# Attention with a gated MLP on one core: the score and pooling stages of pairs 2 and 3, the form of batch 0's v and u products, and a new order of all tasks

## The chip, the core and the metric

The kernel runs on one core of one Trainium2 chip. A core has TensorE (matrix products into PSUM), VectorE (DVE in the profile), ScalarE (ACT), GpSimd (POOL) and SyncE (SP), which issues the transfers between the chip's memory and SBUF. Each engine works through its own list of instructions in order; semaphores tie the lists together. The metric is the device time of one execution in microseconds (us), the median of three runs; a profiled execution is one more run with its own time.

## The reference, cut to what matters

Eight batches; for each, eight heads of 576 positions and 64 dimensions. An attention over pooled q, k, v (groups of four positions) and a local one (positions less than four apart) are added and give x of 576 x 512. A gated MLP follows.

```python
factor = 4; Sd = 144; scale = 1 / 8
q_d = q.reshape(B, H, Sd, factor, D).mean(axis=3)      # k_d, v_d likewise
out_up = np.repeat(sm_attn(q_d, k_d, v_d), factor, axis=2)
mask = np.abs(pos[:, None] - pos[None, :]) < factor
attn = softmax(np.where(mask, scale * q @ k.T, -1e9))
x = out_up + attn @ v                                   # (B, S, H * D)
h = gelu(x @ w_in)                                      # 512 -> 1024
u, v = h[..., :512], h[..., 512:]
v_n = (v - mu) / np.sqrt(var + 1e-06) * g_ln
v_s = np.einsum('ts,bsd->btd', w_sg, v_n) + b_sg[None, :, None]
out = x + (u * v_s) @ w_out
```

## The kernel before

Two heads make a pair; there are 32 pairs, four to a batch, numbered 0 to 31 over all batches. `attention(b, p)` makes the tasks of a pair, `mlp(b)` those of a batch. All tensors lie transposed so that a pair fills 128 partitions.

A pair g runs through these tasks: `lq`, `lk`, `lv`, `lw` load q, k, v in pooling form (`v4`) and v in window form (`vw`); `qs` and `ks` sum q and k over four positions; `S` (L617) is the local score product, 20 plain fp32 products of 64 x 64 x 64, and `Y` (L643) the pooled one; `mx`, `nx`, `my`, `ny` take maxima and biases; `ea`, `eb`, `ec` are the exps; `re`, `rc` sum and invert; `np`, `nq` normalise; `T`, `U`, `t` turn the probabilities on TensorE and `pa` to `pe` evict them; `D` (L782, task `av`) multiplies them with v; `oe`, `od`, `xa`, `xb` put both attentions together into x of this pair.

Three constants set a form for the first pairs. For g < EARLY_S the mask goes into PSUM by two bf16 products ahead of the scores, and S and Y are two tasks; later pairs have one task `YS` (both products) and VectorE adds the mask (`ma`, `mb`). For g < EARLY_D the pooled product runs over four slices of v instead of over their sum; later pairs sum v first (`vs`, two adds for each half on GpSimd or one reduce for each on VectorE, L606). For g < WIDE there is one exp over all ten tiles with the maxima subtracted beforehand (`ia`, `ib`) and the row sums taken by VectorE (`es`); later pairs have ten small exps with a bias each. All three constants are 4.

The MLP products keep fp32 accuracy by splitting each operand into a high and a low part of type fp32r and adding three products. So x gets `xh`, `xl` (its halves) and `xc` (the last 64 positions of the low half beside the high ones), and each weight block, which arrives as float64, is rebuilt (`wu`, `wq`, `wb`, `wt`) and then split (`wh`, `wl`). `v0.s` is the product for 128 positions by 512 columns (L906), 12 products, for the last 64 positions 8, whose two halves `va`, `vj` add; for batch 0 it is cut into quarters by pair (`vk s.k`). `u0.i` (L1117) is 12 products of 128 x 128 x 288. Then follow gelu (`vg`, `ua`), the statistics (`vb`, `vp`, `vn`), the spatial product `s`, the gate, and the output product `o`. From batch 1 on, s and o use sums of blocks with fewer products, whose weights are prepared once (`zf` to `zl`, `ta` to `tl`, `be`, `bs`, `gt`) between batch 0 and 1.

The order is written out by hand: ORDER names every task, and `/V`, `/A`, `/P` choose its engine where the first one listed isn't meant. `place` (L66) hands out buffers in that order: eight PSUM banks, ten wide buffers X, 38 buffers R. The list sets each engine's order and SyncE's; a transfer also waits for the sixth one before it (DEPTH). A load can wait for a task: `lv` of the pairs up to 5 waits for D of two pairs before, `lw` for D of four pairs before. WARM (L211) puts products of zeros ahead of S0 (28) and S3 (20).

## Time and profile before

| | us |
|---|---|
| median of three runs (lowest, highest) | 561.27 (560.44, 561.32) |
| the profiled execution's own time | 562.39 |
| its span, first to last instruction | 560.6 |
| TensorE busy | 536.9 (96%) |
| VectorE busy | 483.5 (86%) |
| ScalarE busy | 417.4 (74%) |
| GpSimd busy | 364.0 (65%) |
| mean granted TensorE clock | 0.994 of full |

The span is divided into stretches below. Times in the rows are microseconds unless marked ns. PE is TensorE, PEld its loading of stationary operands (which overlaps it), PEclk the granted clock as a share of 2.4 GHz. Ends of TensorE's products are modelled, so the spacing of products in a dense run says what one costs, and the mean of one says how long it takes from start to end. "issue" as a releaser means that the profile shows nothing that the engine waited for.

### The profile page before, as it was taken

Reading aid. Unit: us, or ns where it says so; the run is one execution under the profiler, and the core shown is the slowest. Engines: PE = TensorE matmul, PEld = TensorE weight load, DVE = VectorE, ACT = ScalarE, POOL = GpSimd, SP = SyncE. Lnnn points to the kernel's source line nnn. Section 1 sums busy time; section 2 is a strip of 40 time slices with the busy share of each in tenths; the row PEclk is TensorE's granted clock in tenths of the full one; section 3 lists DMA queues with packets and bytes.
Section 4 is the critical chain, followed back from the end, with each engine's and each line's share of the span. In section 5 each row is a group of like instructions: output and inputs, shape, how many; then the busy total and the mean of one; then the engine's idle time right before and its main releaser. Section 6 shows DMA issues by size and latency. Waiting matters only on the chain.

```text
span 560.6 us, 17562 instructions
## 1 busy us (share of the span) xinstructions
PE 536.9 (96%) x6864; PEld 499.9 (89%) x6864; DVE 483.5 (86%) x1008; ACT 417.4 (74%) x1384; POOL 364.0 (65%) x441
## 2 busy tenths in 40 slices
PE   6858999999989999999999999999999999999997
PEld 5656899989989899989998899989999899989997
DVE  8967899999999999897879887897889988777665
ACT  4974899989978788679777789784976797735412
POOL 5992988895576776567648288737847665535314
PEclk9988999999999999999999999999999999999999
DMA  8789529123553053141432323411344133100103
GB/s 314 237 234 318 170 82 278 53 67 105 158 176 122 2 154 110 47 136 42 157 108 77 100 90 122 155 45 57 118 144 135 36 101 109 50 1 2 64 21 107
DMA packets 31923, 64.50 MB, mean 115 GB/s; under 512 B 3808, under 2 KB 4832, under 8 KB 31840
## 3 DMA queue, kind: packets, MB, share of 16 engines
q1 hardware_dynamic: 31840, 63.37, 36.0%
q8 instruction: 54, 0.88, 0.7%
q14 instruction: 29, 0.24, 0.1%
HBM read 53.92 MB, written 9.44 MB: 113 GB/s over the span
## 4 chain that ended last, share of the span: by engine, by line
PE 82%; DVE 8%; DMA 6%; issue 3%; ACT 1%; SPq 1%; DVEq 0%; ACTq 0%
PE ps L1114 19%; PE ps L916 17%; PE ps L1068 16%; PE ps L1243 14%; PE ps L792 4%; PE ps L808 3%; PE ps L629 3%; PE ps L731 3%; DMA R<-in_qT_dram 3%; PE ps L650 2%; PE ps L740 2%; DMA R<-in_kT_dram 1%; DMA weight_z<-in_w_in_dram 1%; DMA weight_y<-in_w_in_dram 1%; SPq L240 1%
## 5 line engine op out<-in xcount | busy, mean ns | idle before, releaser
L1114 PE MATMUL ps<-X,weight_z 128*128 128x288 f32 x512 | 109.2, 298 | 1.6 <-DVE X L637 1.6
L916 PE MATMUL ps<-weight_y,X 128*128 128x512 f32 x320 | 97.3, 398 | 0.1
L689 ACT ACTIVATE X<-X,nb 128x64 f32<-128x64 f32 x280 | 93.6, 339 | 1.2 <-DVE nb L668 0.8
L1114 PEld LDWEIGHTS ps<-X,weight_z 128*128 128x128 f32 x512 | 84.1, 188 | 2.2 <-DVE X L637 1.8
L1114 PE MATMUL ps<-R,weight_z 128*128 128x288 f32 x256 | 75.5, 295 | 0.0
L916 PEld LDWEIGHTS ps<-weight_y,X 128*128 128x128 f32 x320 | 58.5, 188 | 12.7 <-ACT R L1142 0.4
L1068 PE MATMUL ps<-wsg_h,R 128*128 128x288 f32 x266 | 58.4, 300 | 0.3 <-ACT pd L711 0.3
L248 ACT CAST R<-R 128x576 fp32r<-128x576 f32 (+2 forms) x77 | 48.0, 646 | 13.7 <-DVE R L1105 5.9
L1250 DVE TENSOR_TENSOR R<-ps,R 128x288 f32<-128x288 f32 x98 | 41.9, 448 | 16.8 <-PE ps L1243 16.6
L689 ACT ACTIVATION_READ_ACCUMULATOR X<-X,nb 128x1 f32 x280 | 53.4, 191 | 0.0
L248 ACT COPY R<-ps 128x464 f32<-128x464 f32 (+4 forms) x94 | 35.0, 412 | 23.2 <-PE ps L731 10.3
L1226 POOL TENSOR_TENSOR R<-R,R 128x576 fp32r<-128x576 f32 x24 | 35.2, 1477 | 26.2 <-ACT R L248 11.7
L916 PE MATMUL ps<-weight_y,R 128*128 128x512 f32 x128 | 50.6, 395 | 0.5 <-DVE R L827 0.5
L1243 PE MATMUL ps<-R,weight_r 128*128 128x288 f32 x336 | 50.3, 297 | 0.0
L1114 PEld LDWEIGHTS ps<-R,weight_z 128*128 128x128 f32 x256 | 48.2, 188 | 0.1
L1243 PEld LDWEIGHTS ps<-R,weight_r 128*128 128x128 f32 x336 | 46.7, 188 | 0.9
L1068 PEld LDWEIGHTS ps<-wsg_h,R 128*128 128x128 f32 x266 | 43.5, 188 | 0.9 <-ACT pd L711 0.6
L1243 PE MATMUL ps<-R,R 128*128 128x288 f32 x252 | 38.6, 299 | 0.8 <-DVE R L470 0.8
L1003 POOL TENSOR_TENSOR R<-R,R 128x512 fp32r<-128x512 f32 (+1 forms) x18 | 24.9, 1393 | 20.9 <-DVE R L248 7.6
L1142 ACT ACTIVATE R<-ps 128x288 f32<-128x288 f32 x64 | 24.5, 412 | 16.8 <-PE ps L1114 15.5
L1243 PEld LDWEIGHTS ps<-R,R 128*128 128x128 f32 x252 | 34.8, 188 | 1.7 <-DVE R L470 1.2
L711 ACT ACTIVATE pd<-ps,nbd 128x144 f32<-128x144 f32 x96 | 35.3, 377 | 0.9 <-DVE nbd L680 0.2
(215 smaller groups left out, 1624.2 us busy)
## 6 DMA issues: line engine op xcount, KB each, us to landing
R<-in_v_dram SPq DMA_DIRECT2D x56, 224.0 KB, 3.6
X<-in_vw_dram SPq DMA_DIRECT2D x32, 320.0 KB, 3.9
R<-in_kT_dram SPq DMA_DIRECT2D x32, 293.0 KB, 3.6
R<-in_qT_dram SPq DMA_DIRECT2D x32, 293.0 KB, 3.1
out_dram<-R SPq DMA_DIRECT2D x28, 288.0 KB, 3.0
R<-in_w_sgT_dram SPq DMA_DIRECT2D x10, 288.0 KB, 3.9
weight_y<-in_w_in_dram SPq DMA_DIRECT2D x4, 512.0 KB, 5.5
weight_z<-in_w_in_dram SPq DMA_DIRECT2D x4, 512.0 KB, 5.3
```

Source lines behind the costliest of these rows:

```text
L248: (nc.scalar.copy if e == "A" else ENG[e].tensor_copy)(**kw)
L689: nc.scalar.activation(out=st["ms"][:, t, :], in_=src, func=AF.Exp, bias=st["nb"][:, t:t + 1], scale=scale, accum_out=sums[par][:, t:t + 1])
L711: nc.scalar.activation(out=pd[:, n], in_=st["sdv"][n].rearrange("p (c k) -> p c k", c=3), func=AF.Exp, bias=st["nbd"][:, n:n + 1], scale=s ...
L792: nc.tensor.matmul(out=out, lhsT=lhsT, rhs=pdt[ks, probs, h * QC:(h + 1) * QC], start=first, stop=last)
L916: nc.tensor.matmul(out=acc, lhsT=r32(l), rhs=r32(weights[f"y{k}"][:, 0, w]), start=(i == 0 and ks[0] == 0), stop=(i == len(ops) - 1 and ks ...
L1003: ENG[e].tensor_tensor(out=r32(dst), in0=vact[s][0][0:n], in1=vh[0:n, 0:DM], op=ALU.subtract)
L1068: nc.tensor.matmul(out=s_bank(j, c), lhsT=r32(l), rhs=r32(r), start=first_in and i == 0, stop=i == len(ops) - 1, skip_group_check=not firs ...
L1114: nc.tensor.matmul(out=acc[:, 0:HALF], lhsT=r32(l), rhs=r32(r), start=(first and n == 0), stop=(last and n == len(ops) - 1))
L1142: nc.scalar.activation(out=gate(i), in_=at["ps", "m", b, "u", i][:, 0:HALF], func=AF.Gelu_apprx_tanh)
L1226: ENG[e].tensor_tensor(out=r32(gl[m]), in0=us[raws[m]], in1=gh[m], op=ALU.subtract)
L1243: nc.tensor.matmul(out=bank(j, c), lhsT=r32(l), rhs=r32(r), start=first and i == 0, stop=i == len(ops) - 1, skip_group_check=not first)
L1250: nc.vector.tensor_tensor(out=x, in0=bank(j, c), in1=x, op=ALU.add)
```

## The change

EARLY_S, EARLY_D and WIDE become 2: pairs 2 and 3 take the later pairs' form (`YS`, mask added by VectorE, ten small exps, v summed first). For batch 0, v and u become one plain fp32 product for each pair instead of three split ones, from x and the rebuilt weights as they are; batch 0 has no `xh`, `xl`, `xc`, and no `va`, `vj`. The low parts of the weights are waited for by batch 1 instead. `nq` may run on ScalarE as three scaled copies, `xc` on ScalarE. ORDER is new throughout; WARM is the same, but no task S3 is left. Over both orders, tasks change engines: `nq` 14 on ScalarE (none before), `xc` 10 on ScalarE (none before), `vb` 36 on ScalarE (29), `np` 25 on GpSimd (19), `qs` and `ks` 27 on GpSimd (21), `vs` 18 on VectorE (16), `pc` 16 on VectorE (10), `xl` 13 on GpSimd (19).

```diff
 ORDER = """
-wy0 wuy0 wqy0/V wby0 wty0 wz3 wqz3 wbz3 lk0 lq0 qs0 S0 mx0 lk1 lq1 S1 ks0/P Y0 lq2 ks1/P ia0 ib0 wuz3 wy1 ea0 mx1 wqy1
...
-wbz0 ea2 T1 pa1 pa0 wtz0 pb0 my2 pc0 small t0 pe0 wby2 wuy2 wty2 ny2 ec2 es2 my3 ny3/V U1 pb1 pc1/V re2 rc2 t1 whz0
-ks4/P ec3 pe1 D0 oe0 es3 wby1 re3 od0 nq2 why2 YS4 wy3 wuy3 lq5 np2 wqy3 qs5 lv2 U2 T2 pa2 wty1 xa0 rc3 why1 nq3 t3 xb0
-np3 wlz0 my4 ny4 t2 pb2/V wby3 ma4 pc2 lv1 lw1 xh0 xl0/P ec4 U3 wly2 T3 pa3 wty3 mb4 pb3/V wz2 pc3/V lk5 pe2 mx4 pe3 ks5
-wqz2 wbz2 wuz2 D1 YS5 ma5 my5 oe1 od1 xa1 xb1 mb5 lw2 mx5 wly0 D2 oe2/V lv4 od2 xh1/V lw3 vk1.0 vk2.0 nx4 eb4 ea4 re4
-rc4 lv3 D3 xa2 xl1 wtz2 whz2 wly1 vk1.1 nx5 vs4 ea5 eb5 xb2 xh2 ny5 nq4 wz1 oe3/V od3 xa3 xb3 xh3 xc0 why3 wly3 ec5
...
+lq0 lk0 ks0 qs0/P S0 mx0 lk1 ks1/P wy0 wqy0 Y0 my0 lq1 ia0 lq2 ib0 qs1/P ea0 ny0 qs2/P lk3 Y1 wby0 es0 my1 lq3 ec0 re0
+lk2 ks3/P S1 qs3 YS3 lv0 wuy0 mx1 wz3 rc0 ia1 ks2/P ib1 ma3 ny1 ec1 mb3 ea1 es1 re1 YS2 wy1 wuz3 mx3 nq0 ma2 t0 np0 T0
+nx3 wqz3 wz0 pa0 lw0 wty0 U0 rc1 ea3 lk4 nq1 mb2 mx2 np1 T1 pb0/V my3 my2 ny2/V wqy1/V wqz0/V ny3/V pc0/V pe0/V nx2 eb2
+lq5 why0/V lq4 t1 wy2 U1 ec2 wby1 lv1 ea2 ec3 re2 lw1 eb3 D0 pa1/V pb1 pc1 wbz0 ks4/P pe1 qs5/P rc2 np2/V lk5 re3/V rc3
+wuz0 nq3/A wqy2 wy3 T2 oe0/V od0 xa0 xb0 qs4/P YS4 ma4 np3 nq2 T3 pa3 wuy2 wtz0 mb4 mx4 nx4 whz0 pa2 wly0 lv2 D1 t2 U2
+ks5/P my4 ny4 wz1 wuy1 wby2 ec4 lv3 pb2 wty1 pc2/V pe2 oe1/V od1 wuy3 vk2.0 vk0.0 U3 vs2 ea4 eb4 xa1 xb1 pb3 pc3/V wty2
+wqy3/V YS5 t3 ma5 mb5 mx5 vk0.1 vk1.0 vs3 my5 ny5 vk3.0 wby3 ec5 vk2.1 vk1.1 pe3/V lw2 wbz3 wty3 why2 wtz3 nx5 D2 oe2/V
+wly2 od2 xa2 xb2 lw3 D3 oe3/V od3 vk3.1 xa3 wuz1 xb3 vk3.2 lq6 lv4 vk2.2 v0.2 re4 rc4 wz2 ea5 eb5 re5/V vk0.2 v0.0 rc5
...
 """
 DEPTH = 6
-EARLY_S, EARLY_D, WIDE, SMALL_O, SMALL_S = 4, 4, 4, 1, 1
+EARLY_S, EARLY_D, WIDE, SMALL_O, SMALL_S = 2, 2, 2, 1, 1
...
+    def unsplit(t):
+        return at["R", "w", t][:, 0:DM]
...
         def norm_d(e):
+            if e == "A":
+                for i in range(3):
+                    nc.scalar.activation(out=st["pdv"][:, i], in_=st["pdv"][:, i], func=AF.Copy,
+                                         scale=st["rc"][:, NT + i:NT + i + 1])
+                return
...
+        if b == 0:
+            return
         add(N("xh"), {"A": 0.64, "V": 0.4}, x_high, [N("xa"), N("xb")], takes=[("X", "xh", g)])
...
-        add(N("xc"), {"P": 0.27}, x_last, [N("xl")])
+        add(N("xc"), {"P": 0.27, "A": 0.25}, x_last, [N("xl")])
...
-        xn = [f"xl{b * NPAIR + p}" for p in range(NPAIR)]
+        xn = [f"{'xb' if first else 'xl'}{b * NPAIR + p}" for p in range(NPAIR)]
...
+                if first:
+                    for k in ks:
+                        l = sb[k]["x"][:, s * P:min(S, (s + 1) * P)]
+                        nc.tensor.matmul(out=acc[0:LEFT] if last else acc, lhsT=l, rhs=unsplit(f"y{k}"), start=k == 0, stop=k == KT - 1)
+                    return
...
+                if first:
+                    acc = buf("ps", "m", b, "u", i)[:, 0:HALF]
+                    for k in range(KT):
+                        l = block(unsplit(f"z{k // 2 * 2 + d}"))[:, k % 2, ds]
+                        nc.tensor.matmul(out=acc, lhsT=l, rhs=sb[k]["x"][:, cs], start=k == 0, stop=k == KT - 1)
+                    return
...
-            w = [f"wly{i}" for i in range(KT)] if first else []
+            w = [f"{'wty' if first else 'wly'}{i}" for i in range(KT)] if b < 2 else []
...
-            if last:
+            if last and not first:
                 add(N("va", s), {"A": 0.58, "V": 0.6}, v_act(s), [N("v", s)], takes=[("R", "v", b, s)])
...
+            z = [f"z{j}" for j in range(KT) if j % 2 == i // 4]
+            w = [f"{'wt' if first else 'wl'}{j}" for j in z] if b < 2 else []
```

## Rows read from the trace of the kernel before

**Rows 1.** Busy time of each engine by stage; the first line names the columns.

```profile
core 0: us, PE busy (x) PEld busy (x) DVE busy (x) ACT busy (x) POOL busy (x), PEclk, DMA share, GB/s
0.00:52.45 52.45, 37.14 (x854) 30.50 (x854) 40.27 (x106) 34.52 (x121) 38.02 (x52) 0.93 0.85 276
52.45:106.50 54.05, 54.05 (x764) 50.40 (x762) 48.64 (x109) 48.95 (x162) 44.79 (x54) 1.00 0.57 165
...
140.00:162.00 22.00, 19.64 (x242) 18.93 (x242) 21.87 (x50) 18.78 (x47) 12.02 (x12) 1.00 0.51 152
162.00:540.00 378.00, 375.35 (x4489) 352.94 (x4488) 326.46 (x662) 279.61 (x935) 237.47 (x290) 1.00 0.28 89
540.00:560.60 20.60, 17.39 (x131) 17.09 (x129) 14.02 (x29) 4.78 (x9) 6.75 (x5) 0.99 0.21 73
```

**Rows 2.** The same view, two tens of the start.

```profile
30.00:40.00 10.00, 4.72 (x131) 4.09 (x131) 6.17 (x13) 8.98 (x40) 10.00 (x9) 0.91 0.95 266
40.00:50.00 10.00, 8.91 (x224) 8.17 (x228) 6.59 (x15) 4.21 (x23) 4.70 (x7) 0.75 0.91 310
```

**Rows 3.** Waits, 0 to 52.45 us: us in total, times, longest.

```profile
PE ps L808 <- issue: 2.6, 2, 1.5
PE ps L650 <- issue: 2.5, 1, 2.5
...
DVE X L637 <- PE ps L629: 3.7, 1, 3.7
```

**Rows 4.** The chain in order of time: start, us, what.

```profile
29.96 5.87 DMA R<-in_kT_dram
```

**Rows 5.** The chain again: dense runs of TensorE, with their number of records.

```profile
57.04 3.51 PE ps L916 x15
...
67.95 0.52 PE ps L731 x5
68.47 0.29 PE ps L740 x3
68.76 6.38 PE ps L1114 x48
75.14 0.56 PE ps L792 x15
75.70 0.53 PE ps L808 x34
```

**Rows 6.** Groups by line and form: records | busy us, mean ns | idle before.

```profile
L629 PE MATMUL ps<-R,R 64*64 64x64 f32 x1280 | 30.0, 223 | 3.2 <-DMA R<-in_qT_dram 2.2 <-DMA R<-in_kT_dram 1.0
```

**Rows 7.** Timeline of TensorE in the start: start, us, instructions merged.

```profile
13.68 2.36 PE L1433 MATMUL ps<-zeros 128*128 128x256 bf16 x20
16.09 0.43 PE L622 MATMUL ps<-mask_sb,ident_sb 128*128 128x256 bf16 x2
...
33.10 1.71 PE L792 MATMUL ps<-R,R 48*64 48x144 f32 x60
...
34.77 0.78 PE L808 MATMUL ps<-R,X 64*64 64x58 f32 x34
```

**Rows 8.** Groups by line and form on GpSimd and ScalarE.

```profile
L613 POOL TENSOR_TENSOR pairs<-R 112x256 f32<-112x256 f32 x24 | 19.0, 791 | 0.0
L614 POOL TENSOR_TENSOR vd<-pairs 112x128 f32<-112x128 f32 x24 | 12.0, 501 | 1.9
...
L689 ACT ACTIVATE X<-X,nb 128x64 f32<-128x64 f32 x280 | 93.6, 339 | 1.2 <-DVE nb L668 0.8
```

**Rows 9.** Transfers issued from 0 to 60 us: number, size, median us to landing.

```profile
R<-in_v_dram SPq DMA_DIRECT2D x6, 224.0 KB, 6.0
```

**Rows 10.** Waits of TensorE, 52.45 to 560 us.

```profile
PE ps L1114 <- DVE X L637: 1.6, 1, 1.6
```

**Rows 11.** Groups by line and form on VectorE.

```profile
L349 DVE RECIPROCAL R<-R 64x512 f32<-64x512 f32 x1 | 3.3, 3349 | 0.0
```

More of the change, by code (lines that the diff above doesn't have):

```diff
@@ L927, in emit @@
                 vact[s] = [v]
-                if s == NS - 1:
+                if s == NS - 1 and first:
+                    total = dict(accum_out=sum5[s][0:LEFT]) if by_scalar(s) else {}
+                    nc.scalar.activation(out=v[0:LEFT], in_=acc[0:LEFT], func=AF.Gelu_apprx_tanh, **total)
+                elif s == NS - 1:
                     copy(e, out=v[0:LEFT], in_=acc[LEFT:P])
@@ L1321, in mlp @@
                     add(f"vk{s}.{k}", {"T": c / KT}, v_mm(s, range(k, k + 1)),
[L1322 to L1323 removed]
+                        xn[k:k + 1] + w[k:k + 1] + ([f"vk{s}.{k - 1}"] if k else []),
+                        takes=[] if k else [("ps", "m", b, "v", s)], gives=[("R", "w", f"y{k}")])
                 add(N("v", s), {"T": c / KT}, v_mm(s, range(k + 1, KT)),
[L1325 removed]
+                    xn[-1:] + w[-1:] + [f"vk{s}.{k}"], gives=[("R", "w", f"y{KT - 1}")])
             else:
@@ L1345, in mlp @@
         for i in range(2 * KT):
-            w = [f"wl{n}{j}" for n in "z" for j in range(KT) if j % 2 == i // 4] if first else []
-            add(N("u", i), {"T": 1.651}, u_mm(i), xn + w, takes=[("ps", "m", b, "u", i)], gives=xs)
+            z = [f"z{j}" for j in range(KT) if j % 2 == i // 4]
+            w = [f"{'wt' if first else 'wl'}{j}" for j in z] if b < 2 else []
+            add(N("u", i), {"T": 1.651}, u_mm(i), xn + w, takes=[("ps", "m", b, "u", i)],
+                gives=[("R", "w", j) for j in z] if first else xs)
             add(N("ua", i), {"A": 0.38}, u_act(i), [N("u", i), None if opens(i) else N("ua", i - (2 if small_o else 1))],
```

224 lines of the change are left out of this document (109 added, 115 removed).

## The prediction

> **What bounds the kernel now.** I read the stages first [rows 1]. From 52.45 us to 540 us TensorE is the bound: busy 54.05 of 54.05 us in the second stage and 375.35 of 378 us in the long one. What it doesn't fill lies in three places: 15.3 us of the first 52.45 us (52.45 less 37.14), 2.4 us between 140 and 162 us, and 3.2 us at the end, where the last output products drain. In the start every resource is loaded (DMA share 0.85, VectorE busy 40.27, ScalarE 34.52, GpSimd 38.02 of 52.45 us), and the loss comes late in it: from 30 to 50 us VectorE falls to 6.17 and 6.59 of 10 us and the granted clock to 0.91 and 0.75 [rows 2]; both lie between the levels of 1.2 and 2.4 GHz, so TensorE ran at 1.2 GHz for part of these stretches, after it had been busy only 4.72 of 10 us. The waits say why [rows 3]: VectorE waits 3.7 us for the score stage of pair 5, and TensorE stands 5.1 us in three gaps that the profile puts down to "issue". The chain leads from that score stage back to a transfer of kT that took 5.87 us from 29.96 us on [rows 4]. In the stretch from 140 to 162 us VectorE is the bound (busy 21.87 of 22 us): TensorE waits there for it [rows 10], behind the one-time preparation of the weights' sums, in which the reciprocal of g alone holds it for 3.35 us [rows 11].
>
> **The change part by part.** The pivot is the last av product that batch 0 needs, task D3; in the trace it ends at 52.45 us, and from there TensorE runs dense. So I price TensorE's work on both sides of D3 and then ask when D3 ends.
>
> Batch 0's v and u in split form are 4 x 12 + 8 = 56 products of 512 columns and 8 x 12 = 96 of 288. Prices, from dense runs [rows 5]: 3.51/15 = 0.234 us and 6.38/48 = 0.133 us, so 13.1 + 12.8 = 25.9 us go. What comes is 20 plain products of 512 columns and 32 of 288, 19,456 columns. The trace has no plain fp32 product of that size. The score lines show that a plain one leaves two records: 20 calls in each of 32 pairs are 640, and 1280 records stand there [rows 6]. The price of a record is bounded from below by the split form's 0.133/288 = 0.46 ns a column, and from above by the small av products: 0.53 us for 34 records of 58 columns, four 64x64 tiles side by side, is 4 x 15.6/58 = 1.07 ns. Nearest are the transposes, one fp32 record each over almost the whole array: 0.52/5 us for 122 columns and 0.29/3 us for 112, 0.85 to 0.86 ns a column [rows 5]. I take 0.852: 38,912 record columns cost 33.2 us, a quarter product of v 0.87 us, a u block 1.96 us. So these two products get 7.3 us dearer (bounds: 8 us cheaper, 15.7 us dearer).
>
> Pairs 2 and 3 lose the four-slice av: D1 in that form runs from 33.10 to 35.55 us [rows 7], some 2.3 us without its tail, against 0.56 + 0.53 us in the later form [rows 5]: 1.2 us each. They lose the two mask products, 0.43 us with their tail [rows 7]; I take 0.4 a pair (0 to 0.8 us). Together 3.2 us. The 20 warm-up products in front of S3 (2.36 us [rows 7]) go too, since no task S3 is left; TensorE waits there in any case, so I price them at nothing; if they held up the clock, the price is that of 1.2 GHz in a sparse stretch, up to 1.5 us.
>
> Ahead of D3 the new order puts seven quarter products of v (6.1 us) where the old one has three (2.1 us); with the 3.2 us saved, TensorE's list up to D3 is 0.8 us longer, in a stretch where it has idle time to spare. Behind D3 there remain 27.1 us of v and u instead of 23.8: **3.3 us more on the path**. If D3 ended where it does now, that would be the whole effect.
>
> When does D3 end? VectorE's entries ahead of D3, counted in both orders at their row prices, come to nearly the same: two row sums, two sums of q, one shift of weights and one x split fewer, more small evictions; 0.7 us less, of 40.27 us busy [rows 1]. With some 2 us before the first data it can't be through before 41.7 us. The narrow exps of pairs 2 and 3 (ten of 339 ns each, some 3.3 us a pair [rows 8]) replace one wide exp; ScalarE drops four splits of x and several casts ahead of D3, and its load there stays as it is. What goes is the wait for pair 5: its k load is now issued ahead of pair 2's v and of the third and fourth vw load, not behind a v load that waits for D0, and the score stage stands later in the list. What is new is a chain: v of pair 3 is loaded only after D1 (SyncE waits for it, and behind it queue the vw loads of pairs 2 and 3, q of pair 6 and v of pair 4), it lands after 6.0 us [rows 9], and then GpSimd sums it in two adds for each half, 2 x (0.79 + 0.50) = 2.6 us [rows 8], before D3 can run. The old order waits for D1 before that load too, but needs no sum. While GpSimd waits for this v, the totals of y3 and z3 and the split of y2 stand behind it; the first two hold up products that come after D3, and TensorE has the other quarters of v to run. With D1 ending as now at 35.55 us, 0.5 us for the issue, 6.0, 2.6 and 1.1 us for D3: 45.8 us. I take 46.5 us, between VectorE's floor of 41.7 and the present 52.45: **6 us earlier** (0 to 9).
>
> All splits of batch 0's x go (eight instructions for the halves and four copies), and the low parts of y and z are needed only by batch 1; norm and statistics move partly to ScalarE (14 and 7 instances), np and q sums to GpSimd. Counted over both orders at row prices VectorE loses some 12 us in all and ScalarE gains some 17, GpSimd stays. ScalarE was busy 18.78 of 22 us where VectorE was the bound, and 279.61 of 378 us later [rows 1], so it has the room. Three of the five low parts of w_sg's sums move from VectorE to GpSimd (12.02 of 22 us busy there). Of the 2.4 us between 140 and 162 us I count **2 us back** (0 to 2.5). The rest of the new order I price at nothing: TensorE is full from 162 us on, and its idle 2.65 us there bound what can be won; a worse order can lose as much.
>
> Sum against the profiled execution: its own time is 562.39 us, 1.8 over the span; 562.39 - 6 + 3.3 - 2 = 557.7 us. The median of the runs shown is 1.1 us below the profiled one, so I predict **556.6 us**.
>
> **The rivals.** (a) *The plain product is dearer.* At the av products' 1.07 ns the 31,744 record columns behind D3 cost 34.0 instead of 27.1 us: 564.6, as a median 563.5 us, slower. It decides from 1.0 ns a column, where the 4.7 us won are eaten. For it: small plain products never run below it; against it: these are short products with a weight load for each 58 columns, and the transposes, longer ones, run at 0.85. (b) *The start doesn't shorten.* If other waits take the place of the k load (the chain through pair 3's v, or TensorE's gaps without a releaser, which lie where the DMA engines are 0.91 busy and more), D3 ends at some 52 us: 562.1 us as a median with the 2 us won later, 564.1 without: no change or slower. The Trainium skill, "Runtime: NRT & Kernel Launch", section "Instruction fetch mechanics", says that an engine fetches its instructions by a DMA queue of its own in blocks, and that this is mostly hidden; by it these gaps wouldn't be fetches. No row here can tell what they are. (c) *The stall in the middle stays*, or another takes its place: 558.6 us, still faster. (d) *The plain product is cheap.* If a record took one column per tick as the split form does, 0.46 ns, the work behind D3 would be 14.6 us: 544 us. Against it stands every row of a plain fp32 product and of the transposes. The Trainium skill's "Perfetto Trace Analysis", section "Engine Utilization", halves TensorE's rate for FP32_LOW_HIGH, which would give about this; its "FP8 and Floating Point Precision", section "TensorE Precision Notes", counts four passes for true fp32, which the rows bear out better (two records of two ticks a column).
>
> **How the numbers follow.** Chances: forecast 0.52 (own range 551 to 560 us), (c) 0.12, (b) 0.18, (a) 0.12, (d) 0.04, the rest mixtures. Within 0.2% of 561.27 us (1.1 us, about what a measurement of this kernel can tell from no change) lies about half of (b) and an edge of the forecast. Faster 0.66, same 0.12, slower 0.22. The range runs from 551 (D3 at VectorE's floor, the stall gone) to 565 us (a or b in full); only (d) and the tails are left out.
>
> **What would show it.** In the profile of the changed kernel: plain records of 512 columns every 0.43 to 0.44 us, two for a product; 20 x 0.87 us for v and 32 x 0.49 us for u; D3's end at 44 to 49 us and TensorE dense from there; the wait of VectorE for pair 5's scores gone; pair 3's v sum on GpSimd right before D3; between 140 and 162 us less than 1 us idle on TensorE. A record above 0.5 us, D3 beyond 51 us, or new idle time of TensorE over 3 us behind 160 us would make it wrong.

## The result, and the profile after

The changed kernel takes **566.8 us** (median of 4 runs, 566.2 to 571.5), the kernel before 561.0 us (560.4 to 561.3) on the same chip: a ratio of 1.0114, 95% interval 1.0083 to 1.0145. It is slower, where 556.6 us were forecast. The profiled execution took 566.89 us, of which 564.67 us are its span.

To see where the time went I cut both spans at the same three events, each the end of a group of products on TensorE: D3 (the pivot of the forecast), D8 (the av product of pair 8, the first of batch 2) and the last spatial product s of batch 1 (the helper at L1068, after L1085), called s1 here; the expectations call these batch 1's score products. The columns are those of [rows 1]. Before:

```profile
0.00:52.52 52.52, 37.21 (x855) 30.56 (x855) 40.27 (x106) 34.52 (x121) 38.02 (x52) 0.94 0.85 276
52.52:107.66 55.14, 55.14 (x821) 51.49 (x821) 49.76 (x111) 50.11 (x168) 45.95 (x54) 1.00 0.56 162
107.66:175.41 67.75, 65.25 (x784) 60.83 (x778) 66.23 (x130) 59.24 (x199) 47.22 (x55) 1.00 0.40 120
175.41:560.61 385.20, 379.34 (x4419) 357.02 (x4418) 327.26 (x663) 273.50 (x899) 232.83 (x282) 1.00 0.27 85
```

And after, with the window of [rows 1] in which the forecast had seen the stall:

```profile
0.00:47.10 47.10, 37.36 (x743) 27.42 (x743) 36.60 (x103) 33.15 (x144) 32.88 (x51) 0.93 0.92 280
47.10:103.54 56.44, 56.44 (x750) 43.80 (x751) 53.75 (x110) 55.25 (x192) 49.55 (x52) 1.00 0.55 175
103.54:179.11 75.57, 69.42 (x798) 64.04 (x794) 69.85 (x126) 59.49 (x200) 46.86 (x56) 0.98 0.35 111
179.11:564.67 385.56, 380.53 (x4418) 357.42 (x4418) 319.61 (x647) 285.94 (x953) 226.32 (x284) 1.00 0.27 86
140.00:162.00 22.00, 19.41 (x242) 18.34 (x241) 21.28 (x42) 18.86 (x46) 10.98 (x14) 1.00 0.38 121
```

The start is 5.4 us shorter, the dense stage to D8 1.3 us longer, the **middle from D8 to s1 7.8 us longer** (75.57 for 67.75), and the rest, two thirds of the kernel, 0.4 us longer. In the middle TensorE has 6.15 us of idle time where it had 2.50, and 4.2 us more of busy time. Of that, 1.9 us are no loss: 14 of batch 0's spatial products, which the old order has ahead of D8, stand behind it in the new one, so that they lengthen the middle and shorten the stage ahead of it (at the dense spacing of some 0.137 us). These are their groups in the middle after; before has none there:

```profile
L1131 PE MATMUL ps<-wsg_h,R 128*128 128x288 f32 x9 | 2.0, 307 | 0.0
L1131 PE MATMUL ps<-wsg_l,R 128*128 128x288 f32 x5 | 1.4, 296 | 0.0
```

The waits of TensorE in that stage, after (engine, line waited for, total, times, longest):

```profile
PE ps L799 <- ACT R L247: 2.2, 2, 1.6
PE ps L799 <- DVE R L247: 1.4, 1, 1.4
PE ps L1085 <- ACT R L1100: 1.1, 1, 1.1
PE ps L738 <- DVE R L1225: 0.5, 1, 0.5
PE ps L652 <- DVE kd L595: 0.4, 1, 0.4
```

Before, it waited there for two things, 1.6 us ([rows 10]) and 0.8 us. Now the av products (L799) of pairs 9, 10 and 11 wait for the copies of their weights out of PSUM. Those copies are late because VectorE is: from 50.2 to 164.7 us no gap of more than 0.40 us stands between two of its records, and the chain that ended last runs through it, here up to the av product of pair 10 (start, us, what):

```profile
148.49 2.10 DVE wst2l L534
150.59 0.37 DVE R L1225
150.96 0.68 DVE R L1034 x2
...
151.72 1.89 ACT R L247 x4
...
153.65 0.35 PE ps L799 x4
```

And its records are longer than they should be. This is the timeline after of VectorE and GpSimd around 111 us (start, us, engine, line, operation):

```profile
109.84 0.47 POOL L616 TENSOR_TENSOR vd<-pairs 112x128 f32<-112x128 f32 x1
110.17 3.11 DVE L549 TENSOR_TENSOR R<-R 128x288 f32<-128x288 f32 x1
110.26 1.30 POOL L423 TENSOR_TENSOR weight_r<-R,weight_r 128x512 fp32r<-128x512 f32 x1
111.51 0.23 POOL L247 CAST X<-R 128x64 fp32r<-128x64 f32 x1
111.70 1.26 POOL L727 TENSOR_TENSOR X<-X,rc 128x640 f32<-128x640 f32 x1
```

A subtraction of 128x288 that takes VectorE 0.45 us elsewhere took 3.11 us, and ended 0.3 us after the last of four GpSimd instructions in a row. To add such delays up, I took for each VectorE instruction its duration less the lower quartile of its operation and shape over all twenty executions, and summed what is over 0.15 us; this is called the stretch below. From D3 to s1 it is 3.6 us before (0.8 up to D8, 2.8 behind it) and **11.1 us after** (1.8 and 9.3). VectorE's busy time from D3 to s1 is 116.0 us before and 123.6 after: without the stretch 112.4 and 112.5, the same.

### The profile page after: what moved, and what is told of

Read it like the earlier page. It is cut to its first block, busy times and chain, and to the rows that moved or that the text cites. A ratio compares the mean times of both kernels' runs of the same rounds, so it can differ in the third digit from the quotient of the medians.

```text
span 564.7 us, 17289 instructions
## 1 busy us (share of the span) xinstructions
PE 543.7 (96%) x6696; PEld 492.7 (87%) x6696; DVE 479.8 (85%) x983; ACT 433.8 (77%) x1484; POOL 355.6 (63%) x441
## 4 chain that ended last, share of the span: by engine, by line
PE 62%; DVE 13%; ACT 4%; issue 1%; DVEq 0%; ACTq 0%
PE ps L1085 15%; PE ps L1131 13%; PE ps L1266 11%; PE ps L930 11%; PE ps L815 2%; PE ps L799 2%; PE ps L631 2%; PE ps L652 2%; PE ps L738 2%; PE ps L747 1%; ACT X L691 1%; DVE vd L612 1%; ACT R L247 1%; DVE R L247 1%; DVE R L1273 1%
## 5 line engine op out<-in xcount | busy, mean ns | idle before, releaser
L691 ACT ACTIVATE X<-X,nb 128x64 f32<-128x64 f32 x300 | 100.3, 339 | 1.9 <-DVE nb L670 1.5
L1131 PE MATMUL ps<-X,weight_z 128*128 128x288 f32 x448 | 95.2, 297 | 0.0
L930 PE MATMUL ps<-weight_y,X 128*128 128x512 f32 x280 | 84.9, 397 | 0.0
L1131 PEld LDWEIGHTS ps<-X,weight_z 128*128 128x128 f32 x448 | 73.6, 188 | 0.7
L1131 PE MATMUL ps<-R,weight_z 128*128 128x288 f32 x224 | 66.0, 295 | 0.0
L930 PEld LDWEIGHTS ps<-weight_y,X 128*128 128x128 f32 x280 | 51.3, 188 | 10.8
L1085 PE MATMUL ps<-wsg_h,R 128*128 128x288 f32 x266 | 57.9, 299 | 0.0
L1266 PEld LDWEIGHTS ps<-R,weight_r 128*128 128x128 f32 x336 | 46.6, 188 | 3.4 <-ACT mv L969 0.8
L1085 PEld LDWEIGHTS ps<-wsg_h,R 128*128 128x128 f32 x266 | 43.7, 188 | 0.2
L247 ACT COPY R<-ps 128x116 f32<-128x116 f32 (+4 forms) x78 | 28.9, 408 | 14.0 <-DVE R L247 6.4
L612 DVE TENSOR_REDUCE vd<-R 112x128 f32<-112x512 f32 x36 | 37.2, 1076 | 0.0
L727 POOL TENSOR_TENSOR X<-X,rc 128x640 f32<-128x640 f32 x25 | 32.1, 1284 | 6.7 <-DVE rc L724 3.5
L247 DVE COPY R<-ps 128x116 f32<-128x116 f32 (+4 forms) x57 | 22.1, 407 | 15.8 <-ACT R L247 11.1
```

The lines of the kernel that those rows point to most:

```text
L247: (nc.scalar.copy if e == "A" else ENG[e].tensor_copy)(**kw)
L612: nc.vector.tensor_reduce(out=vd[:, i], in_=v.rearrange("p f d -> p d f"), axis=AX.X, op=ALU.add)
L691: nc.scalar.activation(out=st["ms"][:, t, :], in_=src, func=AF.Exp, bias=st["nb"][:, t:t + 1], scale=scale, accum_out=sums[par][:, t:t + 1])
L727: ENG[e].tensor_tensor(out=st["ms"], in0=st["ms"], in1=bc_last(st["rc"][:, 0:NT], KB), op=ALU.mult)
L930: nc.tensor.matmul(out=acc, lhsT=r32(l), rhs=r32(weights[f"y{k}"][:, 0, w]), start=(i == 0 and ks[0] == 0), stop=(i == len(ops) - 1 and ks ...
L1085: nc.tensor.matmul(out=s_bank(j, c), lhsT=r32(l), rhs=r32(r), start=first_in and i == 0, stop=i == len(ops) - 1, skip_group_check=not firs ...
```

## The experiments

All runs use the same three events. The table gives the stages of each profiled execution, VectorE's busy time from D3 to s1 with the stretch in it, and the median with the ratio to the kernel before, run beside it (95% interval). The part behind s1 is 384.7 to 386.6 us in all twenty executions, so what each edit does is decided ahead of s1. a1 is the changed kernel itself once more: its middle is 74.1 us for after's 75.6, which is how far two executions of one kernel can differ there.

| kernel | to D3 | D3 to D8 | D8 to s1 | VectorE, of it stretch | median, us | ratio |
|---|---|---|---|---|---|---|
| before | 52.5 | 55.1 | 67.8 | 116.0, 3.6 | 561.0 | |
| after | 47.1 | 56.4 | 75.6 | 123.6, 11.1 | 566.8 | 1.0114 (1.0083 to 1.0145) |
| p1 plain, old order | 51.3 | 62.0 | 67.8 | 114.5, 3.5 | 568.0 | 1.0125 (1.0104 to 1.0146) |
| p2 sums, old order | 58.3 | 56.3 | 67.7 | 117.1, 4.4 | 569.3 | 1.0148 (1.0129 to 1.0167) |
| p3 both, old order | 57.2 | 62.1 | 67.7 | 115.7, 4.3 | 573.3 | 1.0217 (1.0187 to 1.0248) |
| h1 old order from D3 | 50.7 | 64.9 | 67.8 | 114.9, 3.3 | 570.8 | 1.0174 (1.0152 to 1.0197) |
| h2 old order from D8 | 50.7 | 57.6 | 70.0 | 117.1, 4.6 | 566.1 | 1.0063 (1.0033 to 1.0092) |
| f1 after, fills | 50.0 | 58.1 | 67.9 | 115.7, 3.3 | 564.1 | 1.0034 (1.0008 to 1.0060) |
| f2 before, fills | 51.4 | 55.1 | 66.1 | 112.8, 0.9 | 560.4 | 0.9975 (0.9957 to 0.9992) |
| w1 after, zeros | 47.1 | 56.5 | 74.1 | 123.4, 10.8 | 569.1 | 1.0127 (1.0076 to 1.0178) |
| a1 after again | 46.7 | 56.5 | 74.1 | 123.3, 10.7 | 567.0 | 1.0094 (1.0072 to 1.0117) |
| n1 after, no sums | 52.7 | 56.4 | 70.9 | 118.7, 6.3 | 567.8 | 1.0107 (1.0079 to 1.0135) |
| v1 low parts moved | 47.2 | 56.5 | 74.7 | 123.4, 9.0 | 566.8 | 1.0094 (1.0066 to 1.0122) |
| z1 before, no zeros | 50.5 | 55.5 | 67.8 | 116.2, 3.6 | 562.2 | 1.0024 (1.0006 to 1.0042) |
| q1 after, split | 55.7 | 69.2 | 71.0 | 122.0, 7.4 | 583.0 | 1.0390 (1.0355 to 1.0424) |
| r1 after, no reciprocal | 50.4 | 58.1 | 71.3 | 119.1, 10.0 | 566.5 | 1.0101 (1.0045 to 1.0157) |
| r2 before, no reciprocal | 52.0 | 55.5 | 65.0 | 112.3, 2.9 | 558.7 | 0.9947 (0.9928 to 0.9966) |
| x1 g in the start | 56.1 | 56.5 | 65.0 | 109.5, 3.0 | 564.7 | 1.0068 (1.0049 to 1.0088) |
| x2 g behind D4 | 51.1 | 64.5 | 65.0 | 116.7, 4.1 | 567.6 | 1.0112 (1.0088 to 1.0137) |
| x3 g in pieces | 50.0 | 58.8 | 65.5 | 117.3, 4.2 | 562.5 | 1.0015 (0.9997 to 1.0033) |

### The two parts in the old order

p1 (the 14 steps of batch 0's splits leave the order, nothing else moves):

```diff
 old ORDER
-xh0 xl0 xc0 ... xh3 xl3 xc3 va0.4 vj0.4
 (v and u of batch 0 as in the change; EARLY_S, EARLY_D, WIDE = 4, 4, 4)
```

> The kernel before with one part of the change: batch 0's v and u as plain fp32 products (and so no high and low parts of batch 0's x), everything else, the order above all, as before. Theory A (the price of the plain products, 7.3 us more by the forecast, was about right, and the new order is to blame for the miss): some 6.8 us of the 7.3 lie behind the last av product of batch 0, less 0 to 2 us that VectorE, without batch 0's splits, gives back between 140 and 162 us: 565.5 to 568 us. Theory B (the plain products cost far more on the path than their records say, tails and lost overlap): 570 us and more. Theory C (VectorE's relief pays for them): 560 to 563 us. In the trace of after the records cost 0.436 us (512 columns) and 0.249 us (288 columns), which speaks for A.

Measured: 7.0 us more than before. TensorE is dense from D3 to D8 and this stage is 6.9 us longer, the middle is as before:

```profile
51.34:113.39 62.05, 62.05 (x774) 47.49 (x775) 48.29 (x109) 46.44 (x156) 41.34 (x49) 1.00 0.48 145
113.39:181.15 67.76, 65.24 (x784) 60.83 (x780) 66.18 (x130) 59.21 (x199) 47.20 (x55) 1.00 0.40 119
```

So the plain products cost what theory A gave them, and leaving out the splits gives nothing back where TensorE waits for VectorE.

p2 (the other part, the new steps where the old ones stood) and p3 (both):

```diff
-EARLY_S, EARLY_D, WIDE, SMALL_O, SMALL_S = 4, 4, 4, 1, 1
+EARLY_S, EARLY_D, WIDE, SMALL_O, SMALL_S = 2, 2, 2, 1, 1
 old ORDER, for pairs 2 and 3
-S2 ... Y2 mx2 ia2 ib2 ea2 es2 ... D2
+YS2 ma2 mb2 mx2 nx2 ea2 eb2 ... vs2 D2
```

> The kernel before with the other part alone: pairs 2 and 3 with sums of v and with the later pairs' score stage (and no warm-up products ahead of pair 3), in the old order, the replaced steps where the old ones stood, the sum of v right before its av product. Theory A (the 3.2 us of TensorE work that goes is gained as far as the last av product of batch 0 can come earlier): between 557.5 and 561 us. Theory B (the chain load of pair 3's v after D1, sum on GpSimd, av product takes the place of the work saved, or VectorE and ScalarE can't carry the narrow exps): 562 us or more, with the last av product of batch 0 ending later than 52.45 us.

> Both parts together in the old order: what the change would be without its new order and without ScalarE's share of the small work. Theory A (new order to blame): the parts add up, before + 5 (plain) - 0 to 3 (sums) = 563 to 566 us, below after's 566.77; where the new order were worth what the forecast said, it would stand at 565 us or more and after below it. Theory B (parts to blame): 567 us or more.

Measured: p2 takes 8.3 us more, all in the start, as theory B said, though not by the chain it named: TensorE waits 6.1 us for the sums of q, on which the joined score stage now depends, and runs at 1.2 GHz from 20 to 40 us (waits of p2 from 0 to 60 us; then two tens of its start):

```profile
PE ps L652 <- POOL qd L599: 6.1, 2, 5.2
```

```profile
20.00:30.00 10.00, 5.32 (x73) 4.39 (x70) 6.05 (x13) 5.23 (x31) 3.33 (x5) 0.50 0.93 257
30.00:40.00 10.00, 7.38 (x154) 6.73 (x156) 6.07 (x13) 8.81 (x41) 6.78 (x7) 0.50 0.89 259
```

p3 is 12.3 us slower than before and 6.5 us slower than after: theory A, that the parts are sound and the new order loses the time, fell as it stood. In the old order's start the sums cost more than anything; the new order gains there and loses elsewhere, which the next runs part.

### Which half of the new order loses

h1 and h2 follow the new order up to D3 or D8 and the old one, with its engines for the small work, for all steps left:

```diff
-ORDER = new order
+ORDER = new order up to D8, then the old order without what is done
```

> The changed kernel with the new order up to the last av product of batch 0 (task D3) and the old order, with the old engines for the small work, for all that is left. Forecast of theory A (the start won 5.4 us as it should, and what lies behind it, VectorE's and GpSimd's new share between 106 and 172 us, lost it): the start's gain stays and the idle behind it falls back to about what before has: 566.8 less 4 to 6 us = 560.5 to 563 us, and TensorE's idle between 106 and 200 us is 3 us or less, against 6 in after. Rival (the plain products or the earlier start bring the idle, whatever the order behind): 566 us or more, with 6 us idle in that stretch.

> The changed kernel with the new order up to the av product of pair 8 (task D8, 103.5 us in after's trace) and the old order, with the old engines for the small work, for all that is left. The cut lies where both orders have done nearly the same steps. From the runs so far: the stretch from D8's end to the end of batch 1's score products (s1) took 67.8 us in the kernel before and in four kernels with the old order, 75.6 us in after. Theory M (the new order's middle, and not the parts of the change, loses the time): D8 ends at 103.5 us as in after, the middle takes 68 us, and the kernel ends 4 us ahead of before: a median of 556 to 559 us. Rival (what the earlier start wins is lost later whatever the order): 563 us or more.

Measured: with the old order behind it the middle is 67.8 us (h1) and 70.0 us (h2), so the 75.6 us (74.1 in a1) belong to the new order's middle; h2's extra 2.2 us are little more than the products that the new order leaves behind D8 (13 of the 14 stand there in h2, none in h1). In the total neither reached the figure of its theory. In both, D3 ended at 50.7 us, since TensorE stood for 3.1 and 1.7 us within D3 without a releaser (more on this below); and in h1 the cut left TensorE a second gap of 3.1 us at 54.6 us, and a granted clock of 0.92 up to D8. So h1 says nothing on what a good mixture would take, and h2 is still 0.6% slower than before.

### The cause in the middle

f1 and f2 replace GpSimd's elementwise instructions from D8 to D11 by fills, which read nothing:

```diff
+    if Fills.on and name in ("tensor_tensor", "tensor_copy"):
+        nc.gpsimd.memset(out, 0.0)
```

> The changed kernel with GpSimd's elementwise instructions from the av product of pair 8 to that of pair 11 replaced by fills of the same outputs with zero, so that part of the computation is left out (some sums and low parts are zero); nothing else is moved. Theory C (VectorE instructions with both inputs in SBUF stand still while GpSimd reads SBUF; in after these stretched instructions cost VectorE 9.3 us between D8 and s1, in before 2.8 us): the stretch shrinks to 2 us or less, the stage from D8 to s1 from 75.6 to 68 to 70 us, the drop of the granted clock at 167 us goes, and the kernel takes 559 to 562 us. Rival D (the order of VectorE's and ScalarE's own steps holds TensorE up, and the long VectorE instructions are only slow where nothing waits): the stage stays above 73 us, the kernel above 564 us. Fills may also be quicker on GpSimd itself, which is not the bound there (46.9 of 75.6 us).

> The same replacement in the kernel before, between the same two steps, as the control: the part of the computation that is left out is the same. Theory C: 2.8 us of stretched VectorE time go, TensorE's idle time in that stage (2.5 us) shrinks to 1 us or less: 558.5 to 560 us. Rival D: 560.5 to 561.5 us.

Measured: f1's middle is 67.9 us, 7.7 us shorter than after's and 6.1 us shorter than a1's, and TensorE's idle time in it 1.0 us (67.91 less 66.95). In the control f2 it is 1.7 us shorter, with 1.3 us idle, where theory C had 1 us or less. f1, then f2:

```profile
108.09:176.00 67.91, 66.95 (x799) 62.47 (x793) 62.43 (x126) 59.28 (x200) 28.41 (x56) 1.00 0.40 123
106.53:172.63 66.10, 64.76 (x784) 60.78 (x779) 63.05 (x130) 58.86 (x199) 25.84 (x53) 1.00 0.40 122
```

With fills in both, the middles differ by 1.8 us, which is what the 14 products behind D8 take. The stretch behind D8 falls from 9.3 to 1.6 us and from 2.8 to 0.3 us. Theory C holds for the stage; the totals are higher than it said (f2's by 0.4 us), in f1 since its start took 2.9 us more than after's and the stage behind it, at a clock of 0.97, 1.7 us more (its runs spread from 559.6 to 566.1 us). The fills are also shorter on GpSimd (28.4 us of work for 46.9), so an earlier end of GpSimd's own work could be in the gain too. The trace of after speaks against it: GpSimd was idle for 28.7 of the 75.6 us of its middle, no step of GpSimd is in the chain there, and neither VectorE nor ScalarE nor a product of TensorE waits for one (a weight load does once, for 0.7 us).

v1 puts three of the new order's GpSimd steps back on VectorE, w1 keeps TensorE busy in its stalls:

```diff
-tl1 tl4 tl5
+tl1/V tl4/V tl5/V
```

```diff
+WARM: 10 products of zeros ahead of D9, 14 ahead of D10, 8 ahead of s1.07, 4 ahead of D11
```

> The changed kernel with three low parts of the weights' sums (two of 128x576, one of 64x288) on VectorE instead of GpSimd, at the same places of the order. The forecast counted their move to GpSimd among what relieves VectorE: by it VectorE gets 1.8 us back to do, and the kernel takes 1 to 2 us more. Theory C (VectorE stands still while GpSimd reads SBUF for them: three stretched instructions beside them cost 2.2 us): no difference, within 1 us, and VectorE's stretched time between D8 and s1 falls from 9.3 to 7.1 us.

> The changed kernel with products of zeros put where TensorE stalls in the middle: 10 ahead of D9, 14 ahead of D10, 8 ahead of the batch 1 score product that waited 1.13 us, 4 ahead of D11 (a 256-column product of zeros takes some 0.11 us at 2.4 GHz), as the kernel does at its start. Theory K (the stalls at 152 and 164 us let the clock fall to 1.2 GHz for 3.4 us from 167 us on, which costs half of that): the granted clock stays at 2.4 GHz, and the kernel takes 1.7 us less, 565 us. Rival: the zeros hold up the products behind them, or the clock falls all the same: 566.5 to 568 us.

v1: no difference (566.8 for a1's 567.0 beside it), the stretch 1.7 us less, near the 2.2 that theory C had: what the collisions cost less, the work itself costs more. w1's profile shows the granted clock at full speed where after's fell. After, then w1:

```profile
160.00:167.00 7.00, 5.71 (x49) 5.05 (x47) 6.03 (x12) 4.31 (x22) 4.87 (x6) 1.00 0.22 69
167.00:171.00 4.00, 3.61 (x105) 3.51 (x106) 1.00 (x3) 3.10 (x14) 2.76 (x3) 0.57 0.21 52
```

```profile
167.00:171.00 4.00, 3.85 (x124) 3.67 (x124) 2.56 (x8) 3.59 (x17) 3.10 (x3) 1.00 0.32 82
```

In after TensorE had stalled for 1.1 and 0.5 us at 164 and 167 us, and then ran at 1.2 GHz for 3.4 us, which costs at most 1.7 us. w1's middle is 1.5 us shorter than after's, but no shorter than a1's, whose clock fell at another place (122 us), and w1's median is 2.3 us above after's, over runs from 565.5 to 572.2 us. So zeros in the stalls keep the clock up, but theory K's gain isn't shown.

### What the sums are worth, and where it goes

n1 undoes the sums (the later form of pairs 2 and 3 with all that belongs to it: scores, exps, summed v) inside the new order; with a task S3 in the list again, WARM's 20 zeros ahead of it come back too. a1 is after again, on the same chip:

```diff
-EARLY_S, EARLY_D, WIDE, SMALL_O, SMALL_S = 2, 2, 2, 1, 1
+EARLY_S, EARLY_D, WIDE, SMALL_O, SMALL_S = 4, 4, 4, 1, 1
 new ORDER, for pairs 2 and 3
-YS2 ma2 mb2 mx2 nx2 eb2 ea2 ... vs2 D2
+S2 Y2 mx2 ia2 ib2 ea2 es2 ... D2
```

> The changed kernel with one part undone: pairs 2 and 3 again with the score stage, exps and four-slice av products of the early pairs, and the 20 products of zeros ahead of pair 3, everything in the new order. By the forecast's sum TensorE has 3.2 us more to do ahead of the last av product of batch 0, and 2.2 us of zeros. Theory S (the sums are worth their TensorE work in this order): D3 ends at 49 to 51 us and the kernel takes 2 to 4 us more than after beside it. Rival (the chain of pair 3's v and its sum, or VectorE and ScalarE, set D3): D3 ends at 46 to 48 us and the kernel takes the same.

> The changed kernel once more, unaltered, beside the three others of this call, since runs of different calls can have different chips: 566 to 567 us where nothing differs. What it also tells: in the traces so far TensorE's gaps without a releaser ('issue') in the first 55 us stand at the same places of TensorE's list of records, whatever instruction is there: behind records 1193, 1447 and 1701 (254 apart) in the kernel before and in two kernels made from it, and at 1195 or 1445 in five kernels made from either; the first profile of after has none. Theory F (TensorE waits there for the next block of its instructions, which is late when the DMA engines are full): a gap appears at 1445 in some executions of after, which then end 2 to 4 us later; the spread of its runs is 4 us or more. Rival (they belong to certain steps): no gap, spread below 1 us.

Measured: without the sums D3 ends at 52.7 us, 6.0 us later than in a1 and where before has it. So in this order the whole gain of the start hangs on the sums, and it is larger than theory S had it; in the old order the same sums made the start 5.8 us longer (p2), so it takes both. But the kernel is only 0.8 us slower, and the intervals overlap. The middle gives half of the time back (3.1 us) and the part behind s1 0.9; the two spans differ by 2.0 us. n1, then a1:

```profile
52.67:109.11 56.44, 56.44 (x750) 43.80 (x751) 53.30 (x108) 52.79 (x178) 48.62 (x50) 1.00 0.52 164
109.11:180.04 70.93, 67.18 (x798) 62.49 (x793) 65.36 (x126) 59.42 (x200) 46.91 (x56) 1.00 0.40 118
```

```profile
46.66:103.11 56.45, 56.45 (x751) 43.81 (x751) 53.77 (x110) 55.26 (x192) 49.96 (x52) 1.00 0.56 176
103.11:177.16 74.05, 68.70 (x798) 63.83 (x792) 69.57 (x126) 59.39 (x200) 46.93 (x56) 0.98 0.37 113
```

With the same order and the same engines VectorE is 4.2 us shorter busy in the middle of n1 (65.36 for 69.57), since its collisions fall otherwise (stretch 4.5 for 8.9 us). a1's runs lie within 1.1 us, and its profile has no gap of TensorE without a releaser, so the spread that it should have shown didn't come.

z1 takes the 20 zeros ahead of pair 3 out of the kernel before, q1 puts batch 0's split products back into the new order:

```diff
-WARM = {"S0": 28, "S3": 20}
+WARM = {"S0": 28}
```

```diff
 new ORDER
+xh0 xl0/P xc0 ... xh3 xl3/P xc3 behind each xb; why1 wly1 behind vs3, why3 wly3 behind D3; va0.4 vj0.4
```

> The kernel before with only the 20 products of zeros ahead of pair 3's scores left out. The forecast priced them at nothing, at most 1.5 us of lower clock. In the kernel with the sums in the old order, which lacks them too, the granted clock was at half for 27 us from 13.7 us on. Theory Z (they hold up the clock): a longer stretch at 1.2 GHz than the 6.8 us of before, D3 later, 562 to 566 us. Rival: within 0.5 us of before. And theory F: TensorE's gaps without a releaser stay behind records 1193, 1447 and 1701 of its list, which are now steps that stand 40 records later; the rival has them move with their steps, to 1153, 1407 and 1661.

> The changed kernel with the other part undone: batch 0's v and u again as split products (with the splits of x and the low parts they need, put into the new order where they are first used), pairs 2 and 3 with their sums, the new order for all else. In the old order the plain products alone cost 7.0 us. Theory T (TensorE's added work sets the price wherever it stands): 6 to 7 us less than after, 559.5 to 561.5 us. Theory V (VectorE is the bound from 50 to 164 us, so TensorE's work there is nearly free, and the splits load VectorE and GpSimd more): the end of batch 1's scores comes no more than 2 us earlier than in after, 565 us or more.

z1: 1.0 us slower by the medians (interval 0.3 to 2.4 us). The granted clock, 1.00 and 1.00 from 10 to 30 us before, is lower there:

```profile
10.00:20.00 10.00, 5.73 (x166) 4.38 (x158) 9.96 (x25) 7.94 (x24) 9.00 (x14) 0.86 0.84 298
20.00:30.00 10.00, 8.56 (x178) 7.22 (x180) 7.69 (x16) 7.76 (x29) 7.87 (x10) 0.79 0.66 209
```

Its profiled execution isn't slower, though (D3 at 50.5 us for 52.5), so the trace doesn't show where the 1.0 us arises.

q1 decided nothing: TensorE waits 6.7 us from 55 to 95 us for the high and low parts of z, for which my hand-placed order leaves no time. Whether split products in an order made for them, with the sums, would beat the kernel before stays open.

### VectorE's price

r1 and r2 leave out the reciprocal of g; x1 to x3 keep it and move it ahead of D8 in the kernel before:

```diff
-        nc.vector.reciprocal(out=raw, in_=raw)
```

```diff
 old ORDER
-... gr ... gt ... gs (behind D9)
+x1: gr behind small, gt ahead of ma5, gs ahead of my5
+x2: gr behind lk6, gt behind vb0.2, gs ahead of YS6
+x3: gr ahead of vk0.1; the steps of gt one by one ahead of vp0.2, pa5, vh0.3, pb7, sa0.3, pc8; gs stays
```

> The changed kernel without the reciprocal of g (one VectorE instruction of 3.35 us at 129 us; the values behind it are then g and not 1/g, which is the part of the computation left out). In after VectorE runs from 50 to 164 us without a gap above 0.55 us. Theory V (VectorE is the bound up to the end of batch 1's score products): that end comes 2.5 to 3.5 us earlier, and the kernel takes 563 to 564.5 us. Rival (waits between the engines set it, not VectorE's load): 566 us or more.

> The same omission in the kernel before, as the control. There TensorE has 2.5 us of idle time between D8 and the end of batch 1's scores. Theory V: 1 to 2.5 us less, 558.5 to 560 us; the gain can't be more than this idle time. Rival: no change.

> The kernel before with one thing moved: the load of g's row, its reciprocal with the three steps ahead of it (5.1 us of VectorE) and its split stand in the start, the reciprocal where VectorE waits 3.7 us for pair 5's scores, instead of in the stretch between 107 and 160 us. Theory V (VectorE is the bound between the last av product of batch 0 and the end of batch 1's scores): the start gets at most 1.4 us longer (5.1 less 3.7), the 2.5 us of TensorE's idle time in the middle go: 1 to 2.5 us less than before, 558.5 to 560.5 us, which would beat both kernels. Rival (the delay in the start, where the exps of pair 5 wait for VectorE, costs as much as the middle gives back): no change, 561 to 563 us.

> The kernel before with the same steps of g moved (load, reciprocal with the three steps ahead of it, split: 6.2 us of VectorE), but to the place behind the av product of pair 4 (62 us). There TensorE has a dense list that doesn't wait for VectorE soon, and VectorE is busy only 49.8 of the 55.1 us between D3 and D8. Theory V (VectorE's load up to the end of batch 1's scores is the bound, and what lies in its idle time costs nothing): the start stays as in before, TensorE stalls little behind 62 us, and the idle time of 2.5 us in the middle goes: 558.5 to 560 us on a chip where before takes 561. Rival (a block of 6 us of VectorE makes TensorE wait wherever it stands): 561 us or more.

> The kernel before with the steps of g cut in pieces and laid where VectorE waits for TensorE between D3 and D8 (idle there 1.01 us at 61 us, 0.69 at 68, 0.35 at 85, 0.40 at 95, 0.31 at 97, 0.84 at 104): the three steps ahead of the reciprocal at the first two, the reciprocal in four pieces of 128 columns (a quarter of 3.35 us each) at the other four; the split of g stays. Theory V: no piece is more than 0.6 us longer than the idle time it fills, so TensorE, which is dense there, isn't held up; the stage from D8 to the end of batch 1's scores takes 65 us instead of 67.8, as in the three kernels without these steps in it: 558 to 559.5 us where before takes 561 to 561.7. Rival (VectorE's results come late all the same): 560.5 us or more.

r2 is 2.8 us faster than before, its middle 2.7 us shorter, and TensorE has 0.2 us of idle time left in it:

```profile
107.42:172.44 65.02, 64.86 (x785) 60.77 (x780) 62.27 (x129) 58.93 (x198) 46.53 (x55) 1.00 0.41 124
```

r1's middle is 2.8 us shorter than a1's; its median, 566.5 us, is where the rival had it and not theory V, but says little, as its runs spread from 564.6 to 570.9 us and the profiled one lost 2.6 us within D3. So VectorE's load is the price in the middle of both kernels, at some 0.8 us a microsecond. x1, x2 and x3 all got the shorter middle that theory V said (65.0, 65.0, 65.5 us), and all lost it again ahead of D8: x1 in the start (D3 at 56.1 us), x2 because a release of PSUM stood behind the moved block, and x3, in pieces, in the stage to D8, which took 58.8 us for 55.1. The waits of TensorE in x2 from 50 to 180 us:

```profile
PE ps L917 <- DVE X L638: 6.8, 1, 6.8
```

From D3 to s1 x3 took 124.3 us where before took 122.9. At the three places tried, what VectorE has to do ahead of s1 was paid for wherever it stood, and no version that does the whole computation beats the kernel before.

## Why the prediction was wrong

**The price of the plain products: right.** Records of 512 columns come every 0.436 us (6.11/14) and those of 288 every 0.249 us (3.99/16), where 0.436 and 0.245 were forecast. The timeline after; the next record behind the first row starts at 53.14 us, behind the second at 62.98 us:

```profile
47.03 6.28 PE L923 MATMUL ps<-R,R 128*128 128x512 f32 x14
...
58.99 4.06 PE L1142 MATMUL ps<-R,R 128*128 128x288 f32 x16
```

p1 prices both products behind D3 at 6.9 us; the forecast's prices give 6.9 too, with two quarters of v ahead of D3. That is the one slip: the old order has two there, not three, so that 2.6 us more lie behind D3 after the change, and not 3.3.

**The end of D3: right in its figure (47.1 us for 46.5), wrong in its reasons.** The gain was put down to pair 5's k load, now issued earlier; n1 has that order too, and ends D3 at 52.7 us. It is the sums within this order that bring it. Nor was the chain of pair 3's v what set D3: GpSimd had that sum done at 42.2 us, and D3 began 3 us later, right behind D2. And the gaps without a releaser [rows 3], 5.1 us before, are absent from after's profile, in part by luck: of the eight executions with this start, f1, h1, h2 and r1 have one within D3 and end it at 50.0 to 50.7 us, the other four at 46.7 to 47.2. The zeros, priced at nothing up to 1.5 us, were worth 1.0 us in z1's medians.

**The middle: this step failed.** "Of the 2.4 us between 140 and 162 us I count 2 us back (0 to 2.5)." From D3 to s1 before takes 122.9 us; with 3.3 us of products more and 2 us back it should have been 124.2. It was 132.0, and between 140 and 162 us TensorE has 2.6 us of idle time, where less than 1 was to show the forecast right. These 7.8 us (over the forecast, and as much as the middle's 7.8 over before only by chance) are most of the 9.2 us between the 557.7 us that the sum gave for the profiled execution and 566.89; 0.6 us in the start, 0.4 us behind s1 and 0.4 us around the span are the rest. Two things were wrong in the step.

First, VectorE's relief was counted over the whole kernel and spent in the one stage that needed it. Its busy time fell by 3.7 us in the start and by 7.7 us behind s1, where TensorE is dense and VectorE has time to spare. Between D3 and s1, without the stretch, it didn't change (112.4 and 112.5 us).

Second, work given to GpSimd was taken to be off VectorE's list at full price. GpSimd's busy time is no longer there than before (46.9 us for 47.2), but what it and VectorE do at the same time has changed: from D3 to s1 15 of VectorE's instructions, for 8 before, stand beside GpSimd's with their inputs in SBUF and wait. This added 7.5 us to VectorE's busy time there. f1 takes the cause away, and its middle is longer than f2's by no more than the products that moved there. How the collisions fall is in part chance: n1, with the same order and engines behind D3, has half the stretch in the middle (4.5 us). Through the clock the stalls cost up to 1.7 us more.

**The rivals.** (c), "the stall in the middle stays, or another takes its place", named the place, but let it cost no more than it did before. So the 2.4 us of idle time were taken as the bound of what the new order could do there, as the sentence "a worse order can lose as much" has it for the stretch behind 162 us. Idle time bounds the gain only: with the 2.6 us of products taken off, D3 to s1 lost 6.5 us. (a) and (d) fell with the price. (b) was wrong for this execution, but what it named is real: gaps without a releaser decide in part when D3 ends, and they are fetches of instructions, as the last section shows. None of the rivals let the middle grow, so the range ended at 565 us.

**The rest of the new order at nothing: right** (385.56 us behind s1 for 385.20).

## What to carry to other kernels

Count an engine's relief in the stage where that engine is late, not over the kernel: here 11 us less work elsewhere bought nothing there. Work moved from VectorE to GpSimd isn't off VectorE's list while the two run on operands in SBUF, so look at what stands beside what, and add up how far instructions are longer than their like. And an earlier start is worth only what the next bound lets through: 6.0 us at D3 (n1 and a1) were 0.8 us at the end by the medians.
